# Two attention-then-dense layers on one core: rows averaged two blocks at a time, and another bank layout for the last output tile

## The chip, the cores and the metric

The kernel runs on one core of a Trainium2 chip, as one program. The metric is the device time of one execution in microseconds (us); the median of several executions is compared.

The engines are named as in the profile: PE multiplies matrices (PEld is its loading of the stationary operand), DVE, ACT and POOL work element by element, and SP issues the DMAs. PE writes its results to PSUM, which has eight banks of 512 fp32 columns for each of 128 partitions; DVE and ACT read them there. Everything else lies in SBUF or in HBM.

## The reference

`x` has 2048 rows of 640. Two identical layers follow each other. A layer is linear attention with 32 heads of 20 columns, then a dense block with the Mish activation:

```python
def _A_ref(x, wqkv, w_phi, wo):
    ...
    phi_q = jnp.concatenate([_softmax(pq, axis=-1), _softmax(-pq, axis=-1)], axis=-1)
    phi_k = jnp.concatenate([_softmax(pk, axis=-1), _softmax(-pk, axis=-1)], axis=-1)
    kv = jnp.einsum("bhsf,bhsd->bhfd", phi_k, v)
    z  = jnp.einsum("bhsf->bhf", phi_k)
    num = jnp.einsum("bhqf,bhfd->bhqd", phi_q, kv)
    den = jnp.einsum("bhqf,bhf->bhq", phi_q, z)[..., None] + 1e-6
    o = num / den
    return (lambda x, *d: x.transpose(*d))(o, 0, 2, 1, 3).reshape(B, S, D) @ wo
...
for _ in range(2):
    x = x + _A_ref(_layernorm(x, axis=-1), A_wqkv, A_w_phi, A_wo)
    x = x + _B_ref(_layernorm(x, axis=-1), B_w1, B_b1, B_w2)
```

(The loop stands for two written-out repetitions.) `kv` and `z` need all 2048 rows of a layer before the first `num` can be formed. So each layer has a first attention stage, which makes `phi_q`, `phi_k`, `kv` and `z`, and a second one, which averages: it forms `num`, `den` and `o`, multiplies by `wo` and adds to `x`.

## The kernel before, in words

**Tiling.** The rows are cut into 8 blocks of 256 (`NB`), each of two tiles of 128 rows (`BT`). Each weight and each activation that meets it is split into a high and a low part, and three products (high-high, high-low, low-high) are summed in PSUM, so every multiplication by a weight is three matmuls.

**PSUM.** There are two kinds of tiles. `mm_tile()` (L68) takes two neighbouring banks and has two buffers; `one_tile()` (L71) takes one bank and has four. That is all eight banks. A buffer is given to its next user when its last reader is done.

**The first attention stage** (`attend_first`) computes the features, sums `kv` over all rows into one bank, and writes `phi_q`, turned, to HBM, one tensor `e_d[b]` for each block. Its last tiles are finished inside the second stage: the generator `rest` (L619) hands out their remaining steps, one for each call of `tail()` (L671), which also puts its DVE work behind the last average's multiplication (`div`).

**The second attention stage** (`attend_second`, L666) is where most of the change lies. In it the order of PE and of SP is the order of the program text; the order of DVE, ACT and POOL comes from a planner that simulates the timeline. `load(b)` (L639) fetches the turned features of a block with three DMAs into two "big" tiles and one "ol" tile. `average(b, t)` (L676) averages one tile of 128 rows: eleven groups of heads in turn, each with a weight tile of `kvb`, and each in two halves of 64 rows that go to partitions 0 to 63 and 64 to 127 (L686). All eleven fit in the two banks of one `mm_tile`. Then DVE adds the epsilon (L695, twice), takes the reciprocal (L696) and multiplies (L699, twice); the result is a `row_tile` (four buffers). `Transposed(...).all()` turns a block's two row tiles in ten transposes, two column groups to a bank (L325); ACT copies the high part and DVE subtracts to get the low part (L331). `Rows(b, t).half(c, ps)` (L713) multiplies one tile by half of `wo` (15 matmuls, L391) into one bank; DVE adds it to `x` (L716) and takes statistics (L717). When both tiles are through, DVE forms the mean (L721), POOL two scales and a power (L304, L305), and DVE the shift (L307). SP then writes the block's new `x` (L783), and `fetch` (L432) brings a later one into the buffer that this frees.

**Order of the blocks before.** Blocks 0 and 1 are averaged ahead of the loop. In turns 1 and 2 of the loop the next block (2, then 3) is averaged at the start of the turn; in turns 2 to 5 the block after that (4 to 7) is averaged in the middle, behind the transposes of block b + 1 and ahead of the second tile's products. Each time it is one block, so two tiles.

**The dense block** (`dense`, L795) runs over 8 blocks and 6 pairs of hidden tiles. `hidden` multiplies by `w1` (30 matmuls, L809) into a `one_tile`, `mish` follows on ACT, DVE and POOL (its last steps make the high part `ah`, L834 on ACT, and the low part `al`, L835 on POOL), and `contract` (L837) multiplies by `w2` (24 matmuls of 320 columns, L851) two steps later (`SKEW`). The output of a block's two tiles is summed over all six pairs in two `mm_tile`s, one for each 128 rows, with one bank for each half of the 640 columns. Here the planner orders all engines. `end` (L854) adds the sums to `x` on DVE and writes the result. For the last block of the last layer it does so by halves: four additions (L861), then one DMA for the first tile (L865) and two for the second (L863). For the last pair of the last block the order of the matmuls is hidden tile, then row tile, then half, so the two row tiles end close to each other.

Of the kernel before, what the change touches and what calls it, by code (L numbers as in the profile page):

```python
# [1 line left out]

# [9 lines left out]
ALU = mybir.AluOpType  # L12
# [4 lines left out]
P = 128  # L17
# [27 lines left out]
def kernel(  # L45
# [620 lines left out]
    def attend_second(x_src, x_dst, acc, fetches, makes, fetch_next, begin_next):  # L666
        kva, o_ws, loaded, rest = acc
        rows = {}
        div = [None]

        def tail():  # L671

            with tc.issue_after(div[0]):
                next(rest, None)

        def average(b, t):  # L676

            phs = loaded[b]
            po = mm_tile()
            for g in range(G):  # L680
                n = 120 if g < 10 else 80
                w = GW if g < 10 else 42
                c, j = divmod(g, 8)
                for q in range(2):
                    s0 = t * P + 64 * q
                    nc.tensor.matmul(  # L686
                        po[64 * q:64 * q + 64, c, GW * j:GW * j + w], phs[g][:n, s0:s0 + 64],
                        kvb[:n, g, :w], start=True, stop=True)
            o = row_tile()
            den = work.tile([P, H], F32, tag="r", name="den", bufs=2)  # L690
            pv = [po[:, c, :(DH + 1) * n].rearrange("p (h d) -> p h d", d=DH + 1)
                  for c, n in ((0, 24), (1, 8))]
            hh = (slice(0, 24), slice(24, H))
            for c in range(2):
                nc.vector.tensor_scalar_add(den[:, hh[c]], pv[c][:, :, DH], DEN_EPS)  # L695
            nc.vector.reciprocal(den, den)  # L696
            for c in range(2):
                n = hh[c].stop - hh[c].start
                ins = nc.vector.tensor_tensor(o.rearrange("p (h d) -> p h d", d=DH)[:, hh[c]], pv[c][:, :, :DH],  # L699
                                        den[:, hh[c]].unsqueeze(2).to_broadcast([P, n, DH]), op=ALU.mult)  # L700
                div[0] = ins.ins
            rows.setdefault(b, []).append(o)
            if t == BT - 1:
                del loaded[b]

        class Rows:


            def __init__(self, b, t):
                self.t, self.xt, self.ps = t, xs[b], None  # L710
                self.bn = work.tile([P, 2, 6], F32, tag="bn", name="bn", bufs=2)

            def half(self, c, ps):  # L713
                project_half(ps, cur, self.t, o_ws, 0, c)
                part = self.xt[:, self.t, c * HC:(c + 1) * HC]
                nc.vector.tensor_tensor(part, ps[:, :HC], part, op=ALU.add)  # L716
                nc.vector.bn_stats(self.bn[:, c], part)  # L717

            def mean(self):
                mv = work.tile([P, 2], F32, tag="mv", name="mv", bufs=3)  # L720
                nc.vector.bn_aggr(mv, self.bn)  # L721
                return mv

        with tc.manual_schedule(engines={mybir.EngineType.PE, mybir.EngineType.SP}):
            kv = finish_kv(kva)
            next(rest)
            next(kv)
            loaded[1] = load(1)
# [12 lines left out]
            loaded[3] = load(3)  # L741

            def averages(b):
                for t in range(BT):
                    average(b, t)

            def phi(b):
                if b < NB:
                    loaded[b] = load(b)

            for b in range(NB):
                if b == NB - 1:
# [12 lines left out]
                r0.half(1, one_tile())  # L765
                mv0 = r0.mean()
                if b == NB - 2:
                    ahead = begin_next()
                if b < 2:
                    r1.half(0, one_tile())  # L770
                if b + 1 < NB:
                    nxt = Transposed(rows.pop(b + 1)).all()
                if 2 <= b < NB - 2:
                    averages(b + 2)
                    phi(b + 4)
                if b == 2:
                    tail()
                if b >= 2:
                    r1.half(0, one_tile())
                r1.half(1, one_tile())  # L780
                norm_scale(b, [mv0, r1.mean()])
                xt = xs.pop(b)
                nc.sync.dma_start(row_block(x_dst, b), xt)  # L783
                makes[b]()
                if b + 1 < NB:
                    fetches[b + 1]()
                tail()
                if b < NB - 1:
                    cur = nxt
            for _ in rest:  # L790
                pass
        return ahead


    def dense(x_src, x_dst, w1s, w2s, first, last):  # L795
# [39 lines left out]
            nc.gpsimd.tensor_tensor(al[:, js], n, ah[:, js].bitcast(F32), op=ALU.subtract)  # L835

        def contract(b, pr, ah, al):  # L837
            if pr == 0:
                blocks[b][2] = [mm_tile() for _ in range(BT)]
            pys = blocks[b][2]  # L840
            order = [(t, j) for t in range(BT) for j in range(2)]
            if b == NB - 1 and pr == KF // 2 - 1:
                order = [(t, j) for j in range(2) for t in range(BT)]
            for t, j in order:
                sl = slice(t * P, (t + 1) * P)
                f = 2 * pr + j
                for c in range(2):
                    cs = slice(c * HC, (c + 1) * HC)
                    wh, wl = w2s[f][0][:, cs], w2s[f][1][:, cs]
                    for n, (l, r) in enumerate(((ah, wh), (ah, wl), (al, wh))):  # L850
                        nc.tensor.matmul(pys[t][:, c, :HC], l[:, j, sl], r,  # L851
                                         start=(f == 0 and n == 0), stop=(f == KF - 1 and n == 2))

        def end(b):  # L854
            xt, _, pys = blocks.pop(b)
            dst = row_block(x_dst, b)
            if last and b == NB - 1:
                for t in range(BT):
                    for c in range(2):
                        cs = slice(c * HC, (c + 1) * HC)  # L860
                        nc.vector.tensor_tensor(xt[:, t, cs], pys[t][:, c, :HC], xt[:, t, cs], op=ALU.add)  # L861
                        if t == BT - 1:
                            nc.sync.dma_start(dst[:, t, cs], xt[:, t, cs])  # L863
                    if t < BT - 1:
                        nc.sync.dma_start(dst[:, t], xt[:, t])  # L865
                return
            mvs = []
            for t in range(BT):
                nc.vector.tensor_tensor(xt[:, t, :].rearrange("p (c d) -> p c d", c=2), pys[t][:, :, :HC],
                                        xt[:, t, :].rearrange("p (c d) -> p c d", c=2), op=ALU.add)  # L870
# [152 lines left out]
```

## Time and profile before

| what | value |
|---|---|
| median of 3 executions | 1363.8 us (1362.54 to 1365.35) |
| the profiled execution, whole | 1361.69 us |
| its span, first to last instruction | 1359.7 us, so 2.0 us lie around it |
| granted TensorE clock | 0.999 |
| busy share: DVE, ACT, POOL | 78%, 42%, 34% |
| 252 to 356 us, second attention stage of layer 1 | PE busy 104.00 us of 104, DMA share 0.86 |
| 912 to 1018 us, the same stage of layer 2 | PE busy 105.44 us of 106, DMA share 0.86 |

All rows of the trace come from the one profiled execution. A row of the timeline has the start in us from the span's start, the duration in us, the engine, the line of the kernel, the operation, what is written and what is read, the shapes, the count and, in brackets, the idle time ahead of it with what ended it. A row of the chain of waits has start, duration and what ran. A matmul's end in the trace is modelled, and a matmul that follows another begins before that end; so the pace of PE is read from starts, not from durations.

### The profile page before, as it was taken

What the parts mean: (1) busy time and instruction counts of PE and PEld (TensorE: products, weight loads), DVE (VectorE), ACT (ScalarE), POOL (GpSimd) and SP (SyncE); (2) the same over time, 40 slices, a digit from 0 to 9 for tenths busy, and PEclk for the clock granted to TensorE, in tenths of its full rate; (3) what the DMA queues carried; (4) which work ended last, traced back from release to release, by engine and by line L of the source; (5) the groups of instructions that cost most, each with busy time, mean ns of one, the idle gap of its engine ahead of it and who ended that gap; (6) DMA issues with size and microseconds to landing.
All of it is one profiled execution on the core that took longest, in us unless ns stands there. A gap on an engine that the chain in (4) does not pass through costs nothing.

```text
span 1359.7 us, 30969 instructions
## 1 busy us (share of the span) xinstructions
PE 1349.6 (99%) x12896; PEld 1338.2 (98%) x12896; DVE 1057.4 (78%) x1799; ACT 576.0 (42%) x967; POOL 464.0 (34%) x417
## 2 busy tenths in 40 slices
PE   9999999999999999999999999999999999999998
PEld 9999999999999999999999999999999999999998
DVE  5888988876687887778769788779668776676775
ACT  4444344322454545445443334332236444444443
POOL 2355644444222222222225555634351211111111
PEclk9999999999999999999999999999999999999999
DMA  9543443797714442244563534559964221233200
GB/s 338 156 103 79 98 96 81 206 287 274 222 40 98 117 117 69 61 106 100 145 209 81 119 79 91 96 120 289 289 246 125 78 72 39 86 98 97 73 26 20
DMA packets 352629, 174.11 MB, mean 128 GB/s; under 512 B 287449, under 2 KB 324041, under 8 KB 352489
## 3 DMA queue, kind: packets, MB, share of 16 engines
q1 hardware_dynamic: 352489, 172.14, 46.7%
q8 instruction: 101, 1.65, 0.5%
q14 instruction: 39, 0.32, 0.1%
HBM read 106.23 MB, written 65.86 MB: 127 GB/s over the span
## 4 chain that ended last, share of the span: by engine, by line
PE 94%; DVE 3%; POOL 1%; ACT 0%; issue 0%; DVEq 0%; POOLq 0%
PE mm L391 25%; PE mm L851 25%; PE one L809 25%; PE one L391 12%; PE mm L686 3%; PE one L325 2%; PE one L464 2%; DVE r L425 1%; DVE m L416 0%; DVE r L419 0%; POOL big L427 0%; DVE big L417 0%; DVE r1l L276 0%; POOL xtl L331 0%; POOL r L427 0%
## 5 line engine op out<-in xcount | busy, mean ns | idle before, releaser
L851 PE MATMUL mm<-r2h,ol 128*128 128x320 f32 x1280 | 304.8, 309 | 0.0
L835 POOL TENSOR_TENSOR ol<-big,ol 128x512 fp32r<-128x512 f32 (+1 forms) x98 | 131.1, 1338 | 477.2 <-ACT ol L834 419.1
L809 PE MATMUL one<-xtl,r1h 128*128 128x256 f32 x960 | 268.2, 279 | 0.0
L809 PE MATMUL one<-xth,r1l 128*128 128x256 f32 x960 | 268.0, 279 | 0.0
L809 PE MATMUL one<-xth,r1h 128*128 128x256 f32 x960 | 265.9, 279 | 0.0
L851 PEld LDWEIGHTS mm<-r2h,ol 128*128 128x128 f32 x1280 | 219.2, 188 | 0.0
L851 PE MATMUL mm<-r2l,ol 128*128 128x320 f32 x640 | 197.3, 309 | 0.0
L391 PE MATMUL mm<-r1h,xth 128*128 128x304 f32 (+1 forms) x600 | 185.1, 309 | 1.5 <-DVE r1l L276 1.5
L391 PE MATMUL mm<-r1l,xth 128*128 128x304 f32 (+1 forms) x600 | 183.8, 306 | 0.0
L391 PE MATMUL mm<-r1h,xtl 128*128 128x304 f32 (+1 forms) x600 | 183.5, 306 | 0.2 <-POOL xtl L331 0.2
L809 PEld LDWEIGHTS one<-xtl,r1h 128*128 128x128 f32 x960 | 180.4, 188 | 0.0
L809 PEld LDWEIGHTS one<-xth,r1l 128*128 128x128 f32 x960 | 180.4, 188 | 0.0
L809 PEld LDWEIGHTS one<-xth,r1h 128*128 128x128 f32 x960 | 179.6, 188 | 0.0
L824 DVE TENSOR_SCALAR big<-big 128x512 f32<-128x512 f32 (+1 forms) x98 | 56.6, 578 | 110.0 <-ACT big L822 109.8
L851 PEld LDWEIGHTS mm<-r2l,ol 128*128 128x128 f32 x640 | 120.2, 188 | 0.0
L834 ACT ACTIVATE ol<-big 128x512 fp32r<-128x512 f32 (+1 forms) x98 | 60.9, 622 | 137.8 <-DVE big L833 137.8
L826 ACT ACTIVATE big<-big,two 128x512 f32<-128x512 f32 (+1 forms) x98 | 70.1, 716 | 116.0 <-DVE big L825 115.9
L822 ACT ACTIVATE big<-one,b1s 128x256 f32<-128x256 f32 x192 | 80.9, 468 | 88.5 <-PE one L809 88.0
L427 POOL TENSOR_TENSOR r<-r,r 128x1280 f32<-128x1280 f32 x32 | 77.2, 2413 | 119.1 <-DVE r L426 101.6
L391 PEld LDWEIGHTS mm<-r1h,xth 128*128 128x128 f32 x600 | 112.8, 188 | 2.6 <-DVE r1l L276 1.7
L391 PEld LDWEIGHTS mm<-r1h,xtl 128*128 128x128 f32 x600 | 112.8, 188 | 0.4 <-POOL xtl L331 0.4
L391 PEld LDWEIGHTS mm<-r1l,xth 128*128 128x128 f32 x600 | 112.8, 188 | 0.1
(142 smaller groups left out, 3118.0 us busy)
## 6 DMA issues: line engine op xcount, KB each, us to landing
e_d<-r SPq DMA_DIRECT2D x128, 160.0 KB, 4.0
big<-e_d SPq DMA_DIRECT2D x32, 640.0 KB, 7.6
x_d<-xt SPq DMA_DIRECT2D x23, 640.0 KB, 3.8
xt<-x_d SPq DMA_DIRECT2D x22, 640.0 KB, 5.5
n_d<-xn SPq DMA_DIRECT2D x168, 80.0 KB, 2.3
xt<-in_x SPq DMA_DIRECT2D x16, 640.0 KB, 4.4
xn<-x_d SPq DMA_DIRECT2D x28, 320.0 KB, 4.4
v<-n_d SPq DMA_DIRECT2D x30, 256.0 KB, 3.1
```

Source lines behind the costliest of these rows:

```text
L325: nc.tensor.transpose(ps[:, c, t * P:(t + 1) * P], self.rows[t][:, (c0 + c) * P:(c0 + c + 1) * P], ident)
L391: nc.tensor.matmul(ps[:, :w], a[:, sl], r, start=(k == 0 and n == 0), stop=(k == KD - 1 and n == 2))
L427: nc.gpsimd.tensor_tensor(eg, eg, r.unsqueeze(2).to_broadcast([P, 2 * H, DH]), op=ALU.mult)
L464: nc.tensor.matmul(kva[32 * j:32 * j + DH + 1, 40 * r:40 * r + 40], v[:, (DH + 1) * h:(DH + 1) * (h + 1)], e[:, 40 * h:40 * h + 40], start ...
L686: nc.tensor.matmul(po[64 * q:64 * q + 64, c, GW * j:GW * j + w], phs[g][:n, s0:s0 + 64], kvb[:n, g, :w], start=True, stop=True)
L809: nc.tensor.matmul(ph[:, j, :], l, r, start=(n == 0), stop=(n == 3 * KD - 1))
L822: exps[0] = nc.scalar.activation(part(ta, 0)[:, j - js.start], ph[:, j, :], AF.Exp, bias=b1s[:, 2 * pr + j:2 * pr + j + 1]).ins
L824: nc.vector.tensor_scalar_min(e, e, E_CAP)
L826: nc.scalar.activation(r, n, AF.Ln, bias=two)
L834: nc.scalar.activation(ah[:, js], n, AF.Copy)
L835: nc.gpsimd.tensor_tensor(al[:, js], n, ah[:, js].bitcast(F32), op=ALU.subtract)
L851: nc.tensor.matmul(pys[t][:, c, :HC], l[:, j, sl], r, start=(f == 0 and n == 0), stop=(f == KF - 1 and n == 2))
```

## The change

**In the second attention stage** four tiles are averaged in a row, those of blocks b + 1 and b + 2, at the start of turns 1, 3 and 5. Nothing is averaged in turns 2 and 4, nor in the middle of any turn. The loads of the two blocks that come next are both issued in the odd turns, behind the first half product. The work ahead of the loop stays as it is. Of the four tiles, the first, second and fourth use an `mm_tile`, and the third uses two `one_tile`s.

**In the last block of the last layer** the first row tile sums in an `mm_tile` and the second in two `one_tile`s. For the last pair the 24 matmuls are put in a fixed order, each behind the one before: all of the first row tile, then the first half of the second row tile, then its second half. In the first row tile the products with the low part of the second hidden tile come last.

```diff
-        def average(b, t):
+        def average(b, t, single=False):
 
             phs = loaded[b]
-            po = mm_tile()
+            if single:
+                po = [one_tile(), one_tile()]
+            else:
+                mm = mm_tile()
+                po = [mm[:, 0], mm[:, 1]]
...
             def averages(b):
-                for t in range(BT):
-                    average(b, t)
+                for n in range(2):
+                    for t in range(BT):
+                        average(b + n, t, (n, t) == (1, 0))
...
-                elif b in (1, 2):
+                elif b % 2:
                     averages(b + 1)
...
-                if b in (1, 2):
+                if b % 2:
                     phi(b + 3)
+                    phi(b + 4)
...
-                if 2 <= b < NB - 2:
-                    averages(b + 2)
-                    phi(b + 4)
...
         def contract(b, pr, ah, al):
+            ends = last and b == NB - 1
             if pr == 0:
-                blocks[b][2] = [mm_tile() for _ in range(BT)]
+                if ends:
+                    mm = mm_tile()
+                    blocks[b][2] = [[mm[:, 0], mm[:, 1]], [one_tile(), one_tile()]]
+                else:
+                    blocks[b][2] = [[mm[:, 0], mm[:, 1], mm] for mm in (mm_tile() for _ in range(BT))]
...
+            final = pr == KF // 2 - 1
+            every = range(3)
+            order = [(t, c, j, n) for t in range(BT) for j in range(2) for c in range(2) for n in every]
+            if final and ends:
+                order = [(0, c, 0, n) for c in range(2) for n in every]
+                order += [(0, c, 1, n) for c in range(2) for n in (0, 1)] + [(0, c, 1, 2) for c in range(2)]
+                order += [(1, c, j, n) for c in range(2) for j in range(2) for n in every]
+            elif final and b == NB - 1:
+                order = [(t, c, j, n) for j in range(2) for t in range(BT) for c in range(2) for n in every]
+            before = None
+            for t, c, j, n in order:
                 f = 2 * pr + j
...
+                with (tc.issue_after(before) if before is not None else nullcontext()):
+                    ins = nc.tensor.matmul(pys[t][c][:, :HC], (ah, ah, al)[n][:, j, t * P:(t + 1) * P], w,
+                                           start=(f == 0 and n == 0), stop=(f == KF - 1 and n == 2))
+                if final and ends:
+                    before = ins.ins
```

`phi(b)` issues `load(b)` if there is a block b. Here `t` is the row tile, `c` the half of the output columns, `j` the hidden tile of the pair, and `n` the product: 0 high-high, 1 high-low, 2 low-high. The order of all other pairs is what it was.

More of the change, by code (lines that the diff above doesn't have):

```diff
@@ L1 @@
-from contextlib import ExitStack, contextmanager
+from contextlib import ExitStack, contextmanager, nullcontext
 import concourse.bass as bass
@@ L686, in average @@
                     nc.tensor.matmul(
-                        po[64 * q:64 * q + 64, c, GW * j:GW * j + w], phs[g][:n, s0:s0 + 64],
+                        po[c][64 * q:64 * q + 64, GW * j:GW * j + w], phs[g][:n, s0:s0 + 64],
                         kvb[:n, g, :w], start=True, stop=True)
@@ L690, in average @@
             den = work.tile([P, H], F32, tag="r", name="den", bufs=2)
-            pv = [po[:, c, :(DH + 1) * n].rearrange("p (h d) -> p h d", d=DH + 1)
+            pv = [po[c][:, :(DH + 1) * n].rearrange("p (h d) -> p h d", d=DH + 1)
                   for c, n in ((0, 24), (1, 8))]
@@ L837, in contract @@
         def contract(b, pr, ah, al):
+            ends = last and b == NB - 1
             if pr == 0:
-                blocks[b][2] = [mm_tile() for _ in range(BT)]
-            pys = blocks[b][2]
[L841 to L845, printed above, removed]
-                f = 2 * pr + j
[L847 to L852, printed above, removed]
+                if ends:
[3 more added lines that the diff above has]
+                    blocks[b][2] = [[mm[:, 0], mm[:, 1], mm] for mm in (mm_tile() for _ in range(BT))]
@@ L860, in end @@
                         cs = slice(c * HC, (c + 1) * HC)
-                        nc.vector.tensor_tensor(xt[:, t, cs], pys[t][:, c, :HC], xt[:, t, cs], op=ALU.add)
+                        nc.vector.tensor_tensor(xt[:, t, cs], pys[t][c][:, :HC], xt[:, t, cs], op=ALU.add)
                         if t == BT - 1:
```

3 lines of the change are left out of this document (2 added, 1 removed).

## Prediction

> **What bounds the kernel now.** I read the page first: the busy shares and the chain that ended last.
>
> ```profile
> span 1359.7 us, 30969 instructions
> PE 1349.6 (99%) x12896; PEld 1338.2 (98%) x12896; DVE 1057.4 (78%) x1799; ACT 576.0 (42%) x967; POOL 464.0 (34%) x417
> ...
> PE 94%; DVE 3%; POOL 1%; ACT 0%; issue 0%; DVEq 0%; POOLq 0%
> ```
>
> PE is busy for 99% of the span and holds 94% of the chain. So what PE saves inside the stages comes off the end, as long as no other engine is late in its place. Then the chain in order of time, in layer 2's second attention stage (start, duration, what):
>
> ```profile
> 927.65 1.09 PE one L325 x10
> 928.74 2.20 PE one L391 x15
> ...
> 952.12 2.70 PE mm L686 x88
> 954.82 9.00 PE one L391 x60
> 963.81 1.09 PE one L325 x10
> 964.90 2.70 PE mm L686 x88
> 967.60 9.00 PE one L391 x60
> ```
>
> There is no gap: each piece starts where the last one ends. One half product takes 2.20 us for 15 matmuls, 0.147 each. Behind an averaging piece (L686) the same matmuls cost more: 60 take 9.00 where 60 x 0.147 = 8.80 is due. Behind the transposes (928.74) there is no such extra. The weight loads of the same place show both sides of the averaging:
>
> ```profile
> 963.51 1.16 PEld L325 LDWEIGHTS one<-ident,xn 128*128 128x128 f32 x10
> 964.83 1.25 PEld L686 LDWEIGHTS mm<-kvb,big 120*64 120x64 f32 x40 [0.17 <-PE one L325]
> ...
> 966.11 1.25 PEld L686 LDWEIGHTS mm<-kvb,big 120*64 120x64 f32 x40
> ...
> 967.53 0.19 PEld L391 LDWEIGHTS one<-r2h,xth 128*128 128x128 f32 x1
> ```
>
> From the first tile's loads to the second's it is 966.11 - 964.83 = 1.28 us; that is what a tile takes when another tile follows. The period of a turn is 967.60 - 954.82 = 12.78 us. Of this, 8.80 are the products, 1.09 the transposes and 2 x 1.28 = 2.56 the two tiles. The rest, 0.33 us, is the price of going into the averaging and out of it.
>
> The Trainium skill (TensorEngine Tiling (Array Packing), section Tiling Modes) says that a change of the tiling mode, not just of the tile, drains TensorE. The averaging writes 64 columns at a time, its neighbours 128, so by that rule 0.33 us is no wait for data and goes with the switch; the idle 0.17 us ahead of the loads fits it.
>
> **The change, part by part.**
>
> *Fewer groups.* Per layer there were six groups of two tiles in the loop (turns 1 and 2 at the start, 2 to 5 in the middle); now there are three of four. The number of tiles, products and transposes is the same. Three groups fewer in each of two layers, at 0.33 us: 6 x 0.33 = **2.0 us off**. The three groups removed from the middle now leave the transposes next to products, which costs nothing (928.74).
>
> *The last output tile.* These rows are from the timeline of the end:
>
> ```profile
> 1351.59 0.74 POOL L835 TENSOR_TENSOR ol<-big,ol 128x256 fp32r<-128x256 f32 x1 [0.81 <-ACT ol L834]
> ...
> 1354.83 0.31 PE L851 MATMUL mm<-r2h,ol 128*128 128x320 f32 x1
> ```
> ```profile
> 1354.59 1.69 DVE L861 TENSOR_TENSOR xt<-mm,xt 128x320 f32<-128x320 f32 x4 [3.53 <-PE mm L851]
> ...
> 1355.90 0.92 SPq L863 DMA_DIRECT2D out<-xt  x2
> ```
>
> DVE idles for 3.53 us, then does all four additions in a row, 1.69 us, about 0.40 from one start to the next. The fourth starts at 1354.59 + 3 x 0.40 = 1355.79, though the last matmul ended at 1354.83 + 0.31 = 1355.14. With the new order the 24 matmuls of the last pair start at 1354.83 - 23 x 0.147 = 1351.45. The first row tile ends with the 12th, at 1351.45 + 11 x 0.147 + 0.31 = 1353.38; its two additions run until about 1354.2. The first half of the second tile ends with the 18th, at 1354.26, and is added until 1354.75. For the last half DVE is then free at 1355.14, and its addition starts there, 1355.79 - 1355.18 = **0.6 us** sooner; its DMA and the end follow it. The bounds: if the two halves of the second tile are still released together, the last addition starts one addition later, and 0.2 us is left. If the last DMA also lands faster because the others have gone 0.6 us or more ahead, at most another 0.5 us comes off, half of the 0.92 us that two issues take.
>
> The new order needs the low part of the second hidden tile at the 11th matmul, 1351.45 + 10 x 0.147 = 1352.92; POOL has it at 1351.59 + 0.74 = 1352.33. The 0.6 us between them cover it. Without that cover PE stalls for whatever is missing.
>
> *Banks and DVE.* What is new is four tiles in a row with no cover for DVE. The rows of turn 1, where DVE is fullest, since the steps of `rest` run there too:
>
> ```profile
> 930.76 1.50 DVE L478 STREAM_TRANSPOSE r<-r 128x1280 f32<-128x1280 f32 x1
> ...
> 934.29 0.25 DVE L695 TENSOR_SCALAR den<-mm 128x24 f32<-128x24 f32 x2
> 934.57 0.35 DVE L696 RECIPROCAL den<-den 128x32 f32<-128x32 f32 x1
> 935.78 0.23 DVE L307 SCALAR_TENSOR_TENSOR stats<-mv,stats 128x1 f32<-128x1 f32 x2 [0.86 <-POOL stats L305]
> ...
> 940.49 0.48 DVE L716 TENSOR_TENSOR xt<-one,xt 128x320 f32<-128x320 f32 x1
> ...
> 945.86 0.17 DVE L695 TENSOR_SCALAR den<-mm 128x24 f32<-128x24 f32 x1
> ...
> 947.44 0.25 DVE L695 TENSOR_SCALAR den<-mm 128x24 f32<-128x24 f32 x2
> ```
>
> A tile takes DVE 947.44 - 945.86 = 1.58 us against 1.28 on PE. The fourth tile needs the first one's banks, 3 x 1.28 = 3.84 us after the group began. In turn 1 the group begins at 928.74 + 2.20 = 930.9, and the first tile was through at 934.3, 3.4 us later: 0.4 us to spare. The third tile takes two of the four single banks; the first half product takes another, and by then the older ones are read. Tighter is what comes next. Two more tiles are 3.2 us more DVE work ahead of the addition that ran at 940.49. It is due when its product ends: the group and three half products after 930.9, 4 x 1.28 + 0.33 + 6.60 = 12.05, so at 942.95. DVE gets to it at 940.49 + 3.2 = 943.7, or 942.8 if the 0.86 us wait for POOL is filled. The next half product, which reuses that bank, starts one set of transposes later, at 944.0. So it waits for 0 us at best and, with the 0.48 us of the addition and no idle time filled, for 0.1; if the 1.5 us turn (L478) is put in front, for 1.6. I take 0.1 us per layer, **0.2 us on**, nearest to the plain order, and keep 0 and 1.6 as ends. Turns 3 and 5 have no `rest` work of that size: nothing.
>
> *Loads.* SP gets six loads in turns 1 and 3 instead of three, ahead of the turn's weight fetch and its write of `x`.
>
> ```profile
> big<-e_d SPq DMA_DIRECT2D x32, 640.0 KB, 7.6
> x_d<-xt SPq DMA_DIRECT2D x23, 640.0 KB, 3.8
> xt<-x_d SPq DMA_DIRECT2D x22, 640.0 KB, 5.5
> ```
>
> They are issued one half product into the odd turn, and wanted at the next odd turn. An odd turn takes 4 x 1.28 + 0.33 + 9.89 = 15.3 us, an even one 9.9, so 25.2 - 7.7 = 17.5 us remain, against 7.6 for a big load and twice that if two blocks come one behind the other. The buffer of `x` goes through a write and a fetch, 3.8 + 5.5 = 9.3 us, between the end of one turn and the first addition two turns on: 9.9 + 5.4 + 2.2, or 15.3 + 2.2, each 17.5 us; before, it was at least 15.0. Both are covered; I count nothing.
>
> *Sum:* -2.0 - 0.6 + 0.2 = **-2.4 us**. The profiled execution took 1361.69 us, of which its span is 1359.7; with the change that span should be about 1357.3. The median of the runs is 2.1 above the profiled execution, and the same 2.4 off it gives **1361.4 us**. That is 0.18%. A measurement of this kernel can tell about 0.2%, 2.7 us, from no change, so the edge to "faster" lies at 1361.1 and the one to "slower" at 1366.5.
>
> **The rivals.**
>
> *DVE too late in turn 1.* By the Trainium skill (TensorEngine Tiling (Array Packing), section Performance Considerations), tiling speeds up TensorE but not the reading of PSUM, which can become the bottleneck. The rows agree with that in size, 1.58 us on DVE against 1.28 on PE. As a mechanism here: the half product behind the transposes waits for its bank, 0.5 to 1.6 us in turn 1 of each layer. -2.6 + 2 x 1.0 gives 1363.2, and the far end, -2.6 + 3.2, gives 1364.4. For it speaks that DVE has hardly a gap there; against it, that the same work is done by the same time and only its order changes.
>
> *The shift of the statistics (L307) in front of the first tile: slower.* The planner may put DVE's wait for POOL ahead of the first tile's additions. How long this can be:
>
> ```profile
> 978.84 0.23 DVE L307 SCALAR_TENSOR_TENSOR stats<-mv,stats 128x1 f32<-128x1 f32 x2 [3.28 <-POOL stats L305]
> ```
>
> The last addition takes 0.48 us; its statistics are another pass over the same columns, so with the mean I estimate 1.2 us into the group. A wait of 3.28 and the shift end at 4.7, the first tile at 6.3, where 3.84 is needed. So PE stalls for about 2.4 us. It decides from the point at which DVE begins the first tile later than 3.84 - 1.58 = 2.3 us into the group. In turns 3 and 5 of both layers that is 4 x 2.4 - 2.6 = +7.0, **1370.8 us**. Against it: in turn 1 the shift stood behind the second tile's reciprocal (935.78).
>
> *More than counted.* The last DMA lands faster too, by up to 0.5 us, and no stall appears: -2.6 - 0.5 gives 1360.7.
>
> *The end does not follow.* The halves are released together: -2.0 - 0.2 + 0.2 gives 1361.8.
>
> **How the numbers follow.** The forecast has 0.52, DVE too late 0.18, the slower rival 0.12, more than counted 0.13, the end that does not follow 0.05. The forecast lies 0.3 us from the edge to "faster", and the three runs of before spread over 2.8, so I put half of it, 0.27, below the edge. Faster: 0.27 + 0.13 = 0.40. Slower: 0.12, and 0.02 for the first rival with a stall in turn 3 as well, 0.14. The rest, 0.46, is within 0.2%. The range goes from 1359.6 (the best case, less some of that spread) to 1364.6 (the far end of the first rival, rounded up); outside lie the slower rival and a little below.
>
> **What would show it.** In the chain of waits the averaging pieces of turns 1, 3 and 5 should hold 176 matmuls in about 5.3 us, with 9.9 us for products and transposes behind the 0.2 us of the way out; the even turns should run without an L686. There should be no idle time on PE behind the transposes of turn 1 (first rival) or ahead of the fourth tile (second). At the end the last addition should start within 0.1 us of the last matmul's end, with a gap ahead of it on DVE. The prediction is wrong if the price of a group does not fall with the number of groups, or if PE idles anywhere for over 1 us where it did not.

## The result: slower, and the profile after

| | before | after |
|---|---|---|
| median, same chip | 1363.62 us (1362.28 to 1365.35, 7 runs) | 1369.62 us (1366.16 to 1374.65, 7 runs) |
| ratio | | 1.0049, 95% interval 1.0029 to 1.0069 |
| the profiled execution, whole | 1361.69 us | 1371.52 us |
| its granted clock | 0.999 | 0.996 |
| ahead of the first averaging | 252.0 us | 251.2 us |
| second attention stage, layer 1 | 104.03 us | 110.63 us |
| second attention stage, layer 2 | 105.30 us | 110.81 us |
| last weight load of a hidden tile to the end | 15.50 us | 14.34 us |

The stages are cut in the trace at the first weight load of an averaging and at the first and last of a hidden tile. The sum of the stage differences, -0.8 + 6.6 + 5.5 - 1.2, is 10.1 us, and the spans of the two profiled executions differ by 10.0 (1369.7 - 1359.7). So the loss is in the two averaging stages, some 6 us in each, and the end gained 1.2 us. In the kernel after, lines of this stage stand three or four further down: L686, L695, L696, L699, L716 and L783 are now L690, L699, L700, L703, L720 and L786.

The page of the kernel after: its span, busy shares, and the chain that ended last.

```profile
span 1369.7 us, 30985 instructions
PE 1353.6 (99%) x12896; PEld 1342.1 (98%) x12896; DVE 1059.1 (77%) x1799; ACT 575.6 (42%) x967; POOL 463.8 (34%) x417
...
PE 84%; DVE 5%; POOL 3%; DMA 3%; ACT 1%; issue 1%; SPq 1%; POOLq 0%
```

PE's share of the chain fell from 94% to 84%; DVE, POOL and the DMAs took it over. What PE waits for (total us, times, longest), in the kernel after; before had none of these three rows:

```profile
PE mm L690 <- DVE xn L703: 5.6, 2, 3.0
...
PE one L391 <- DVE xtl L331: 1.4, 2, 0.7
...
PE one L391 <- DVE xt L720: 0.7, 2, 0.5
```

The first row is two waits, of 2.6 and 3.0 us, one in each layer, ahead of an averaging tile. Here is that of layer 2, in turn 5. First the weight loads of the four tiles (start, duration), then DVE, then POOL:

```profile
988.85 1.25 PEld L690 LDWEIGHTS mm<-kvb,big 120*64 120x64 f32 x40 [0.19 <-DMA raw<-in_w]
...
990.12 1.25 PEld L690 LDWEIGHTS mm<-kvb,big 120*64 120x64 f32 x40
...
991.41 1.25 PEld L690 LDWEIGHTS one<-kvb,big 120*64 120x64 f32 x40
...
995.86 2.05 PEld L690 LDWEIGHTS mm<-kvb,big 120*64 120x64 f32 x40 [3.08 <-issue]
...
998.21 0.29 PEld L391 LDWEIGHTS one<-r2h,xth 128*128 128x128 f32 x1
...
998.64 0.33 PEld L391 LDWEIGHTS one<-r2h,xtl 128*128 128x128 f32 x1
998.91 0.33 PEld L391 LDWEIGHTS one<-r2h,xth 128*128 128x128 f32 x1
```
```profile
990.38 0.26 DVE L699 TENSOR_SCALAR den<-mm 128x24 f32<-128x24 f32 x2 [0.16 <-PE mm L690]
990.67 0.35 DVE L700 RECIPROCAL den<-den 128x32 f32<-128x32 f32 x1
994.71 0.23 DVE L307 SCALAR_TENSOR_TENSOR stats<-mv,stats 128x1 f32<-128x1 f32 x2 [3.69 <-POOL stats L305]
994.86 0.89 DVE L703 TENSOR_TENSOR xn<-mm,den 128x480 f32<-128x480 f32 x2
```
```profile
989.89 3.74 POOL L164 TENSOR_TENSOR r1l<-raw,r1h 128x640 fp32r<-128x640 f32 x3 [4.28 <-ACT r1h L134]
993.71 0.19 POOL L304 TENSOR_SCALAR ve<-mv 128x1 f32<-128x1 f32 x1
993.99 0.69 POOL L305 TENSOR_TENSOR stats<-ve,neg_half 128x2 f32<-128x2 f32 x1
```

The first three tiles are 1.27 and 1.29 us apart, as forecast. The fourth starts 4.45 us after the third, where 1.28 is due. It needs the banks of the first, and DVE has the first tile's reciprocal at 991.02 but does not multiply: the shift L307 stands in between and waits for POOL, which is making the low part of weights (L164) ahead of its second scale L304. Those weights came late. The chain of waits shows from where:

```profile
978.73 1.94 SPq L647
...
980.72 0.43 SPq L786
...
981.19 7.80 DMA raw<-in_w
...
995.89 2.39 PE mm L690 x44
```

The fetch of the weights is issued behind the loads of two blocks, whose issue ends at 978.73 + 1.94 = 980.67; it starts at 981.19 and lands 7.80 us later. And there is a second part. The fourth tile takes 2.35 us (998.21 - 995.86 from its first weight load to the next line's), not 1.28, and the matmuls behind it come 998.91 - 998.64 = 0.27 us apart, not 0.147. The windows of layer 1 (stretch, its length, busy us of PE, PEld, DVE, ACT and POOL, then granted clock, DMA share, GB/s) say why:

```profile
322.00:326.00 4.00, 3.30 (x114) 3.18 (x110) 1.19 (x5) 0.86 (x2) 3.83 (x5) 1.00 0.98 337
326.00:329.00 3.00, 1.15 (x22) 1.18 (x24) 2.25 (x9) 0.00 (x0) 0.64 (x1) 0.69 1.01 362
329.00:334.00 5.00, 5.00 (x42) 4.92 (x40) 2.99 (x11) 0.00 (x0) 0.00 (x0) 0.50 0.50 205
334.00:337.00 3.00, 3.00 (x23) 3.00 (x23) 1.30 (x3) 0.00 (x0) 0.00 (x0) 1.00 0.02 5
```

Behind the gap PE is granted half its clock, though it is busy. In this execution the half clock lasts 6.83 us in layer 1, from 327.14, and 3.41 us in layer 2, from 996.15. The spread of the seven runs of the kernel after goes with it: the one at a clock of 1.0 took 1366.16 us, the one at 0.995 took 1374.65. That the half clock is all of the spread is not shown, since only one of the seven left a trace. The run at 1.0 was still 2.5 us above the median of before.

The end, in the kernel after: the last additions on DVE, and the last matmuls in the chain.

```profile
1364.63 0.89 DVE L875 TENSOR_TENSOR xt<-mm,xt 128x320 f32<-128x320 f32 x2 [2.36 <-PE mm L863]
1365.51 0.49 DVE L875 TENSOR_TENSOR xt<-one,xt 128x320 f32<-128x320 f32 x1
1366.39 0.49 DVE L875 TENSOR_TENSOR xt<-one,xt 128x320 f32<-128x320 f32 x1 [0.39 <-PE one L863]
```
```profile
1364.60 1.77 PE one L863 x12
```

The last addition starts 0.02 us after the last matmul (1364.60 + 1.77 = 1366.37), with idle time ahead of it, just as the prediction wanted it. From its end, 1366.88, to the span's end at 1369.7 it is 2.9 us; before, it was 1359.7 - 1356.28 = 3.4.

### The profile page after: what moved, and what is told of

The parts are those of the page before. It is cut to its first block, busy times and chain, and to the rows that moved or that the text cites. A ratio compares the mean times of both kernels' runs of the same rounds, so it can differ in the third digit from the quotient of the medians.

```text
span 1369.7 us, 30985 instructions
## 1 busy us (share of the span) xinstructions
PE 1353.6 (99%) x12896; PEld 1342.1 (98%) x12896; DVE 1059.1 (77%) x1799; ACT 575.6 (42%) x967; POOL 463.8 (34%) x417
## 4 chain that ended last, share of the span: by engine, by line
PE 84%; DVE 5%; POOL 3%; DMA 3%; ACT 1%; issue 1%; SPq 1%; POOLq 0%
PE one L812 25%; PE mm L391 24%; PE mm L863 24%; PE one L391 7%; DMA raw<-in_w 2%; POOL r1l L164 1%; PE one L464 1%; PE one L325 1%; DVE r L425 1%; PE mm L690 1%; PE one L863 1%; DVE xn L703 1%; POOL r L427 1%; DVE m L416 0%; DVE r L478 0%
## 5 line engine op out<-in xcount | busy, mean ns | idle before, releaser
L863 PE MATMUL mm<-r2h,ol 128*128 128x320 f32 x1240 | 296.1, 309 | 0.0
L863 PEld LDWEIGHTS mm<-r2h,ol 128*128 128x128 f32 x1240 | 212.5, 188 | 0.0
L863 PE MATMUL mm<-r2l,ol 128*128 128x320 f32 x620 | 191.2, 309 | 0.0
L863 PEld LDWEIGHTS mm<-r2l,ol 128*128 128x128 f32 x620 | 116.4, 188 | 0.0
```

The source lines that it names most:

```text
L863: ins = nc.tensor.matmul(pys[t][c][:, :HC], (ah, ah, al)[n][:, j, t * P:(t + 1) * P], w, start=(f == 0 and n == 0), stop=(f == KF - 1 and ...
```

## The experiments

Theory behind all of them: DVE's shift L307, which waits for POOL, stands in the row of four tiles, holds the first tile's banks and so PE, and half the clock follows. Rivals: the loss is at the end; it is DVE's work on four tiles itself; it is the late loads alone; it is the new third tile in single banks.

### Each half of the change alone

*Before, with the new end only:* `dense` is that of after, `attend_second` that of before.

> The kernel before with the change to the last output tile alone; the averaging stays as before. Theory (the end gains, the averaging loses): the last addition starts 0.6 us sooner after the last hidden matmul, the last DMA lands about 0.5 us faster, and the whole is 1.1 us faster than before, about 1362.5 us. Rival (the two single banks that the last block holds make the hidden products wait): PE idles among the hidden products of the last block, and the whole is slower than before by over 1 us.

Measured: 1362.33 us against 1363.05, ratio 0.9995 (0.9986 to 1.0003). The profiled execution's last 15.50 us became 14.34, and its last additions look like those of after:

```profile
1359.94 0.49 DVE L872 TENSOR_TENSOR xt<-one,xt 128x320 f32<-128x320 f32 x1
1360.82 0.49 DVE L872 TENSOR_TENSOR xt<-one,xt 128x320 f32<-128x320 f32 x1 [0.39 <-PE one L860]
```

The end saves 1.16 us in the trace; the time alone, -0.7 us, can't be told from nothing. Either way the end is not the cause of the loss.

*After, with the old end:* the averaging is that of after, `dense` that of before.

> The changed kernel with the dense block of before; only the averaging is changed. Theory: all of the loss is here, +7 us against before (6 of the whole plus the 1.1 that the end gave), with PE idle for 2.5 to 3.5 us ahead of the fourth tile of turn 5 in each layer and about 1 us at the start of turn 2. Rival (the loss comes from the dense block): within 1 us of before.

Measured: 1374.0 us, ratio 1.0072 (1.0055 to 1.0089), which is some 10 us and more than the 7 expected. The matmuls of the fourth tile of turn 5 start 2.57 and 3.17 us late, the first weight load of turn 2's products 1.0 us late in each layer, and the clock is 0.50 for 3.41 us behind each late fourth tile. All of the loss is in the averaging.

### The shift behind the four tiles

```diff
-                norm_scale(b, [mv0, r1.mean()])
+                mvs = [mv0, r1.mean()]
+                def late(b=b, mvs=mvs):
+                    with tc.issue_after(div[0]):
+                        norm_scale(b, mvs)
+                if b % 2 or b >= NB - 2:
+                    norm_scale(b, mvs)
...
                 elif b % 2:
                     averages(b + 1)
+                    late()
```

> The changed kernel, with the shift and scales of turns 0, 2 and 4 computed behind the four averages that follow, so that DVE's wait for POOL no longer stands ahead of the averages' multiplications. Theory (this wait holds the first tile's banks): the idle time ahead of the fourth tile of turn 5 goes in both layers, 5.9 us in the profile, and with it the half clock that follows, some 4 us; the 1 us at the start of turn 2 stays. The whole comes to 1361 to 1362.5 us. Rival (four tiles in a row outrun DVE and the banks whatever stands in front): the fourth tile still waits for over 2 us and the whole stays at 1368 or more.

Measured: **1359.65 us, ratio 0.9972 (0.9961 to 0.9983)**, faster than both kernels and than the 1361 to 1362.5 expected. POOL's scales and power moved behind the four tiles together with the shift. DVE now does all four tiles in a row and the shift behind them, without a wait:

```profile
983.41 0.89 DVE L703 TENSOR_TENSOR xn<-mm,den 128x480 f32<-128x480 f32 x2
...
987.83 0.89 DVE L703 TENSOR_TENSOR xn<-mm,den 128x480 f32<-128x480 f32 x2
988.75 0.23 DVE L307 SCALAR_TENSOR_TENSOR stats<-mv,stats 128x1 f32<-128x1 f32 x2
```

The averaging stages take 103.28 and 105.15 us, the granted clock is 1.0 all through, the fourth tile never waits, and of the waits at products only 0.26 us are left in turn 2 of each layer (weight load to weight load, less the usual 0.147). Order, tiles, loads and banks of PE are those of after. So neither four tiles in a row, nor the single banks, nor the loads cost the time by themselves. The stages of after less those of this kernel are 7.35 and 5.66 us. In layer 1 the gap ahead of the fourth tile is 2.72 of it (2.78 from one matmul to the next, less the usual 0.06), the waits of turns 2 and 3 are 0.74 and 0.75, and 3.1 remain for the half clock. In layer 2 it is 3.16, 0.73 and 0.48, and 1.3 remain. So by these differences the half clock cost about 4.4 us in that execution. The trace's own figure is near: PE was busy for 6.12 and 3.41 us at half clock, and half of that is 4.8.

*The same with the old end:*

> The averaging of the changed kernel with the shift behind it, and the dense block of before: what the merged groups alone bring. Theory (0.33 us for each of the six groups that are gone): 2.0 us less 0.5 us of waits at the start of turn 2, so 1.5 us faster than before, and 1.1 us slower than the same with the new end, about 1361 us. Rival (the end brings nearly all of the 3.4 us): within 0.5 us of before.

Measured: 1361.87 us, ratio 0.9988 (0.9978 to 0.9998). The averaging with the shift out of the way gains 1.6 us (0.3 to 3.0) by itself; -2.0 was counted for it, and +0.2 for DVE's lateness.

### Other ways to take the wait away

*The loads one block at a time,* so that the weight fetch of an odd turn stands behind three loads, not six:

```diff
-                if b % 2:
+                if b:
                     phi(b + 3)
-                    phi(b + 4)
```

> The changed kernel, with the loads of the turned features issued one block for each of turns 1 to 4 instead of two in turns 1 and 3. Theory (the wait for POOL is that long because the weight fetch of turn 3's end lies behind two blocks' loads): the fetch lands within 5 to 6 us instead of 7.8, POOL makes the low parts sooner, and the wait ahead of the fourth tile of turn 5 falls below 1 us, so about 1363 us. Rival (the loads are not the root; the planner's order of POOL and DVE alone is): the fourth tile still waits for 2 to 3 us and the whole stays at 1367 to 1371 us.

Measured: 1379.01 us, ratio 1.0113 (1.0099 to 1.0127), where 1363 was expected. The step that it was to show is there: in layer 2 POOL begins the low parts 999.02 - 993.02 = 6.00 us after the fetch that turn 3 issues, against 989.89 - 981.19 = 8.70 in the kernel after; in turn 5 the wait at L307 fell from 3.69 to 0.3 us, and the fourth tile did not wait. But block 5's features now come too late for turn 3:

```profile
PE one L690 <- DMA big<-e_d: 10.7, 5, 5.4
```

So the double load does push the weights, and through them POOL and the shift; taking it apart costs more than it saves.

*POOL's power ahead of the weights' low part:*

```diff
-        nc.gpsimd.tensor_tensor(stats[:, b, 0], ve, neg_half, op=ALU.pow)
+        last_pow[0] = nc.gpsimd.tensor_tensor(stats[:, b, 0], ve, neg_half, op=ALU.pow).ins
...
-                makes[b]()
+                with tc.issue_after(last_pow[0]):
+                    makes[b]()
```

> The changed kernel, with POOL's low parts of the weights (L164) held behind the power of the same turn's statistics, so that they no longer stand between the two scales (L304); DVE's order stays as in the changed kernel, with the shift (L307) inside the averages. Theory (DVE waits because POOL does 3.5 us of weights, and a weight fetch before that, ahead of the statistics): DVE's wait for POOL at L307 falls to about 1 us at a time, below what the fourth tile has to spare, PE's wait for the averages' multiplications goes, and the whole comes to 1359.5 to 1361.5 us. Rival (the place of the shift in DVE's order is enough to stall PE, whatever POOL does first): the fourth tile still waits for over 1 us in turn 5, and the whole stays above 1365 us.

Measured: 1384.62 us, ratio 1.0152 (1.0133 to 1.017). The theory's cure failed. (Lines are two further down here: the low part is L166, the power L307, the shift L309.) First DVE, then POOL:

```profile
946.49 3.49 DVE L309 SCALAR_TENSOR_TENSOR stats<-mv,stats 128x1 f32<-128x1 f32 x2
949.90 0.34 DVE L702 RECIPROCAL den<-den 128x32 f32<-128x32 f32 x1
```
```profile
945.75 0.70 POOL L307 TENSOR_TENSOR stats<-ve,neg_half 128x2 f32<-128x2 f32 x1
946.41 3.48 POOL L166 TENSOR_TENSOR r1l<-raw,r1h 128x1536 fp32r<-128x1536 f32 x1
```

POOL has the power early, so DVE hardly waits for it. But the two shifts, 0.23 us elsewhere, now take 3.49 us, just as long as POOL's L166, which begins 0.08 us ahead of them. The Trainium skill (SBUF — State Buffer, section Who interferes with whom) states that a DVE instruction with two inputs in SBUF contends with a GpSimd instruction that reads SBUF; it calls the ports that the two share an exclusive lock, and says that the order of issue decides who blocks. The rows agree: L309 has two SBUF inputs, L166 began first, and L309 ends 0.09 us behind it (949.98 against 949.89). So the wait was turned into a blocked instruction. The rows are of turn 1; in turns 3 and 5 the shifts take 3.45 and 1.56 us inside the first tile, again beside an L166, and the fourth tile starts 3.0 and 1.1 us late.

*The same in the kernel before, meant as a control:*

> The kernel before, with the one line that holds POOL's low parts of the weights behind the statistics. Theory (before the change DVE's wait for POOL cost nothing, since no bank that PE needed hung on it): DVE's waits at L307 fall from 18.3 us in total to below 10, and the time stays within 0.5 us of before. Rival (it cost before too, and taking it away is a gain of its own): 1 us or more faster than before.

Measured: 1370.62 us, ratio 1.0047 (1.0035 to 1.0059). The same collision came here too (the shift took 3.52 us beside an L166 of 3.51), so it controls nothing. What it does show: a shift that holds DVE for 3.5 us *can* cost the kernel before as well, where it falls in turn 1.

*The shift late, and in turn 1 the transposes ahead of both products of the second tile,* to take the last wait of 0.26 us:

```diff
-                if b < 2:
+                if b < 1:
                     r1.half(0, one_tile())
...
-                if b >= 2:
+                if b >= 1:
                     r1.half(0, one_tile())
```

> As the kernel with the shift behind the averages (1359.65 us), and in turn 1 the transposes come ahead of both products of the second tile instead of between them, so that two half products cover the splitting of the next block. Theory (what is left at the start of turn 2, 0.26 us in each layer, is the low part that comes late): it goes, and the whole is 0.5 us faster, about 1359.2 us. Rival (DVE is too full in turn 1, so that the banks come late instead): PE waits as long at another place of turn 1, and the whole is 1359.5 us or more.

Measured: 1360.38 us, ratio 0.9971 (0.996 to 0.9982), no better than without it, as its rival had it. The wait in turn 2 is gone, and one of 0.34 us appears in turn 1 between the transposes and the first product behind them.

### The shift off DVE, in both kernels

The cleanest test is to let POOL form the shift, so that DVE waits for it nowhere, and to do it to both kernels.

```diff
-            nc.vector.scalar_tensor_tensor(stats[:, b, 1, t:t + 1], mvs[t][:, 0:1], -1.0,
-                                           stats[:, b, 0, t:t + 1], op0=ALU.mult, op1=ALU.mult)
+            neg = work.tile([P, 1], F32, tag="neg", name="neg", bufs=2)
+            nc.gpsimd.tensor_scalar(neg, mvs[t][:, 0:1], -1.0, 1.0, op0=ALU.mult, op1=ALU.mult)
+            nc.gpsimd.tensor_tensor(stats[:, b, 1, t:t + 1], neg, stats[:, b, 0, t:t + 1], op=ALU.mult)
```

After, with this edit:

> The kernel after, with the shift of the statistics (L307) computed on POOL, right behind POOL's own power, instead of on DVE. DVE then waits for POOL nowhere in the second attention stage; the order of PE, the loads and the banks are those of after. Theory (a 128x1 shift on DVE, placed by the planner between the first tile's reciprocal and its multiplication, holds the fourth tile): the gaps of 2.8 and 3.2 us ahead of the fourth tile in turn 5 go, the half clock behind them (about 4.2 us in all) goes with them, and the wait of about 1 us at turn 2 shrinks by the 0.87 us that the shift held in turn 1. So after's 1369.6 less 6.0, less 4.2: about 1359.5, between 1359 and 1361.5. Rival (DVE's work on four tiles in a row is itself too much, the shift only stands where DVE is late anyway): PE still waits over 1 us ahead of the fourth tile in turn 5, and the time stays above 1365.

Before, with this edit:

> The control: the kernel before, with the same shift computed on POOL instead of on DVE. DVE's total wait at the shift is 18.3 us in before and 19.8 us in after, nearly the same. Theory (the wait costs only where four tiles stand in a row; with two tiles there are banks for both, and nothing waits for the first): the time stays within 1 us of before's 1363.5, so 1362.5 to 1364.5. Rival (the wait costs before as well, hidden in small pieces, and the gain of the shifted order has nothing to do with the merged groups): before gains 3 us or more, to 1360.5 or below.

Measured: 1369.38 us, ratio 1.0047 (1.0034 to 1.006), and 1371.94 us, ratio 1.0063 (1.0051 to 1.0075). The second time is outside both expectations, and the first is the rival's only in its number, since no averaging tile waited for DVE in either kernel: the averaging stages took 103.36 and 105.15 us in the first, 104.18 and 105.60 in the second. The dense stages, from their first to their last hidden tile, had grown from 326.7 to 330.9 us, in both layers of both kernels, and this is the loss. There the matmuls of the hidden tiles follow each other more slowly, with PE busy throughout. Two weight loads of the first of the two kernels, the first and the last of twelve in a row:

```profile
399.87 0.19 PEld L813 LDWEIGHTS one<-xth,r1l 128*128 128x128 f32 x1
...
401.19 0.19 PEld L813 LDWEIGHTS one<-xtl,r1h 128*128 128x128 f32 x1
```

That is (401.19 - 399.87) / 11 = 0.120 us. The edit adds small POOL instructions and a new tile of 4 bytes for each partition. To tell the two apart, the next pair forms the shift in place, with as many POOL instructions and no tile:

```diff
-            neg = work.tile([P, 1], F32, tag="neg", name="neg", bufs=2)
-            nc.gpsimd.tensor_scalar(neg, mvs[t][:, 0:1], -1.0, 1.0, op0=ALU.mult, op1=ALU.mult)
-            nc.gpsimd.tensor_tensor(stats[:, b, 1, t:t + 1], neg, stats[:, b, 0, t:t + 1], op=ALU.mult)
+            sh = stats[:, b, 1, t:t + 1]
+            nc.gpsimd.tensor_scalar(sh, mvs[t][:, 0:1], -1.0, 1.0, op0=ALU.mult, op1=ALU.mult)
+            nc.gpsimd.tensor_tensor(sh, sh, stats[:, b, 0, t:t + 1], op=ALU.mult)
```

After, in place:

> As the run with the shift on POOL, but POOL forms it in place in stats and no new tile is allocated. In that run the averaging stages took 103.36 and 105.15 us, against 110.63 and 110.81 in after, and the matmuls of the hidden tiles in the dense block came 120 ns apart instead of 117, so that each dense stage took 330.9 instead of 326.7 us. Theory (the added 4-byte tile moved other tiles to other addresses, and the pace of the hidden matmuls went with that): the dense stages are back at 326.7, the averaging stages stay near 103.4 and 105.2, and the time is 1369.4 - 8.4 - 1.4 (the same kind of loss ahead of the first averaging and between the layers) = 1359.6, between 1359 and 1361. Rival (POOL's additional instructions slow PE's reading in the dense block): the dense stages stay at about 330.9, and the time at 1368 to 1370.

Before, in place:

> The same in place in the kernel before, the control: no new tile, L307 on POOL. Theory (the wait of 18.3 us in all that DVE had at L307 held nothing that PE needed; the 8 us that the first form of this control lost were the dense stages, at 330.9 us each): averaging stages as before at 104.0 and 105.3 us, dense stages at 326.7, the time within 1 us of before's 1363.4. Rival (the wait costs before as well): 1360.5 or below. Rival (POOL's instructions slow PE in the dense block): 1370 to 1372.

Measured: **1360.42 us, ratio 0.9974 (0.9964 to 0.9985)**, and 1363.82 us, ratio 1.0005 (0.9995 to 1.0015). The hidden tiles are back at (401.15 - 399.87) / 11 = 0.116 us:

```profile
399.87 0.19 PEld L813 LDWEIGHTS one<-xth,r1h 128*128 128x128 f32 x1
...
401.15 0.19 PEld L813 LDWEIGHTS one<-xth,r1l 128*128 128x128 f32 x1
```

and the chain of waits in layer 2's turns 4 and 5 holds PE alone:

```profile
978.20 4.40 PE one L392 x30
982.60 2.70 PE mm L691 x88
985.30 1.28 PE one L691 x44
986.58 1.28 PE mm L691 x44
987.87 4.60 PE one L392 x30
```

Four tiles in 5.26 us and 30 products behind them in 4.60, which is 0.2 over 30 x 0.147: the picture that the prediction drew. POOL still has its second scale behind the weights, at 988.41, later than the whole group; nothing waits for it.

| | shift on DVE | shift on POOL, in place |
|---|---|---|
| before | 1363.6 | 1363.8 |
| after | 1369.6 | 1360.4 |

The right column was measured in another set of runs; before itself took 1363.3 there. With the shift out of DVE's row the change gains 3.4 us; in before, the same edit does nothing. So the wait at L307, as long as it is in these two kernels, costs only where four tiles stand in a row. That before waited as long is seen in DVE's own waits, first of before and then of after:

```profile
DVE stats L307 <- POOL stats L305: 18.3, 14, 3.3
```
```profile
DVE stats L307 <- POOL stats L305: 19.8, 14, 3.7
```

## Why the prediction was wrong, step by step

**Fewer groups: right.** With the shift out of the way the pieces are what the prediction counted, and the kernel with the averaging alone gained 1.6 us (0.3 to 3.0) where 2.0 was forecast, 0.26 us of wait in each layer's turn 2 included. The trace is sharper: with the shift behind the four tiles the stage of layer 1 took 103.28 us against 104.03, and 0.75 with the 0.26 added is 1.0, three groups at 0.33. In layer 2 it was only 0.15 less, with longer waits for loads in the first tiles of the stage. The Trainium skill's rule that a change of the tiling mode drains TensorE goes with that: three changes fewer, and the time of three went. (The prediction has three groups removed from the middle of a turn; it was all four there and the one of turn 2's start, with two new ones in turns 3 and 5. The count of three fewer is the same.)

**The end: right, and the upper bound came true.** 0.62 us through the earlier last addition (0.6 forecast) and 0.5 us because the last transfer is done sooner, which the prediction had only as a bound: 1.16 us in the trace. The rival "the end does not follow" falls.

**"Turns 3 and 5 have no `rest` work of that size: nothing": this step failed.** It asked only for DVE's work and left out DVE's wait for POOL, which held PE for 2.7 and 3.2 us ahead of the fourth tile of turn 5. That wait was known: the 3.28 us at 978.84 stand in the prediction, under the rival "the shift in front of the first tile", with a chance of 0.12. Its mechanism is what happened: the shift stood not ahead of the first tile but inside it, between the reciprocal and the multiplication, which for the banks is the same. Its place was half right: turn 5 in both layers, 2.7 and 3.2 us against 2.4 forecast; in turn 3 the shift came behind the first tile's multiplication (start 968.33, after 965.32), so no fourth tile waited and only a product did, for 0.5 to 0.8 us. Its time, 1370.8, lies within the spread of the measured runs, but by chance: it had two stalls too many and left out the half clock.

The reason given against it, that in turn 1 of before the shift stood behind the second tile's reciprocal, said where the planner put it in *that* order of PE. It said nothing on the new one, where the planner could put it anywhere between the mean and its use. What was missing is the question of slack: before, a tile had the other buffer and at most one tile behind it; after, the first tile's banks are due 3.84 us after the group begins, and a wait of 3.3 us that the trace already showed would not fit in unless it stood outside. The point from which the rival decides was worked out (2.3 us), but not the chance that an unconstrained instruction falls inside it, with three groups in each layer.

**"I count nothing" for the loads: half wrong.** Features and `x` rows came in time for the four tiles. But the fetch of weights stands behind the two blocks' loads and lands 7.80 us after its issue; POOL's low part, the second scale and the shift follow it. With the loads one block at a time the shift's wait in turn 5 was 0.3 us. The prediction named the fetch as the thing that is queued behind, and then asked only for the rows.

**DVE in turn 1: too small.** 0.1 us per layer was taken; the wait was 1.0 us, at the first product of turn 2, for `xtl` and not for the bank of an addition. 0.74 of it went when the shift of turn 1 (which waited 0.87 us for POOL) was moved, so it is the same cause again; the 0.26 that remain go too when POOL forms the shift.

**The half clock: not thought of.** A stall of PE was priced at its own length. In the profiled execution the half clock that followed cost another 4.4 us or so, and the runs from 1366.2 to 1374.7 us stand nearly in the order of their clocks.

Open: why the planner put the shift just there in turn 5 and not in turn 3. Its own estimate of when POOL is done is not in any trace.

## What to carry to other kernels

When work is merged into longer runs of one engine, each buffer in the run gets a due time; list everything that may stand between its producer and its reader, the short instructions that wait for a third engine above all, and price each of them by the longest wait that the old trace shows for it, even where it held nothing then. An instruction whose place a planner is free to choose should be bound to a place outside the run: with the shift bound behind the four tiles the same change turned from +0.5% to -0.3%. And price a stall of PE with the slower clock that may follow it, not by its length alone.

## What the hardware showed that was not expected

**Half clock after a short gap.** PE's weight loads stood still for 2.65 us in layer 1 and 3.08 us in layer 2, and the granted clock then was 0.50 for 6.83 and 3.41 us: 0.27 us from one product to the next, not 0.147. The Trainium skill (TensorE: Matmul & The Clock Gate, section Part 1: The HAM clock gate) gives one idle window of about 3.4 us as the condition; both gaps here were shorter, and the clock fell all the same. Nor is this bound to the four tiles. In the profiled execution of before with the new end, PE waited 2.2 us for features ahead of layer 2's loop, and the clock was 0.50 for 3.41 us behind it; in that of the late shift with the old end it was 2.6 us of wait and 6.83 us of half clock. And the gap's length alone does not decide: with POOL's power first, a gap of 2.8 us in turn 3 was followed by a clock of 1.0 in layer 1 and by one of 0.50 in layer 2. What decides stays open.

**A blocked instruction looks busy.** The shift of 128x1 took 3.49 us beside POOL's 3.48 and was counted as DVE work, not as a wait. A view of waits alone would have called that kernel cured.

**A tile of 4 bytes and the pace of matmuls.** With it the 128x256 matmuls of the hidden tiles came 0.120 us apart, without it 0.116, in both kernels and both layers. Over all places where one weight load of a hidden tile follows another, the means are 121.0 and 118.4 ns; 2.63 ns for each of 1440 matmuls are 3.8 of the 4.2 us that a dense stage lost. That the tile is the cause is shown, since as many POOL instructions without it cost nothing, and the two kernels with it ran on the same chip as others with dense stages of 326.7 us; that it acts by moving other tiles to other addresses is only argued.
